# A retention layer and a bilinear feed-forward on one core: other zero products, wide state updates and a new order in the first pairs, and one burst two blocks sooner

## The chip, the core and the metric

The kernel runs on one core of a Trainium2 chip. A core has a matrix engine (TensorE, PE in the profile; its weight loads are listed apart as PEld), VectorE (DVE), ScalarE (ACT), GpSimd (POOL) and SyncE (SP), which here only issues transfers. Each engine works through its own queue in order and waits on semaphores that the others raise. Matmul results go to PSUM, from where DVE and ACT read them. The metric is device microseconds for one execution of the program.

## The reference

For 4 batches, 8 heads, 768 positions and head size 64, a recurrent layer keeps a 64x64 state for each head, and its output is the input of a bilinear feed-forward:

```
state = gamma[h] * state + outer(k[t], v[t])      # gamma[h] = 1 - 2**(-5-h)
y[t]  = q[t] @ state / sqrt(64)
x     = y, as 3072 tokens of 512 columns
out   = ((x @ w_a) * (x @ w_b)) @ w_out           # 512 -> 1536 -> 512
```

Inputs and output are float32.

## The kernel before

The 3072 tokens are 24 slots of 128. A slot is made of two chunks of 64 positions, and the recurrence is done chunk by chunk. The decay is put into tables with which k and q are scaled on their way to bf16 (`scaled`, L206). Then a chunk's output is the sum of two things: its masked scores times its values (`intra`), and the state of all earlier chunks times its queries (`inter`). The states are running sums of k-times-v products.

The feed-forward works on tiles of 4, 2, 2, 2, 2, 4, 4 and 4 slots (`TILES`, L16). For each of 12 column groups `ft` there is a product `a`, copied by ACT to bf16 (`asb`, L509), and a product `g`, which DVE multiplies by it into `ht` (L520); then twelve matmuls for each slot give `o` (L545), which ACT copies out. Weights come in six parts, cast by POOL. `a`, `g`, `o`, one of the two tiles of chunk sums and, in the first pairs, some transposes and scores take turns in a ring of three PSUM tiles ("ff", pool `psff`). A tile of the ring can be written only when the reader of the tile three places earlier is done. The other PSUM tiles are "y0", "y1", "at" (two banks) and "st".

The order of every engine's work is the order in which the program calls things: `seq` (L71) ties each instruction to the one before it on its engine. There are two ways in which slots are turned into columns of x.

*The first three pairs of slots (0 to 5)* go through functions ending in 2, called one by one from L559 to L637. A pair holds even positions in one slot and odd ones in the other (`par`). `casts2` scales k and q and casts v; `flip2` (L387) transposes k or q on TensorE into PSUM, and ACT or DVE copies the result to SBUF; `scores2` (L399) makes k-times-q with 64x64 matmuls; `mask2` (L415) is two DVE multiplications of 512 columns into `aT`; `update2` (L422) adds a chunk's k-times-v to the state in PSUM ("st") with sixteen 64x64 matmuls; `keep_state` (L439) has ACT copy its two halves into the off-diagonal-zero matrices `gbd[0]` or `gbd[1]`; `intra2` (L454) and `inter2` (L443) make the output in y0 and y1, or for pair 1 in two tiles of the ring; `leave2` (L466) copies the output's two halves into x, on ACT and DVE. Between these calls `warm` (L481) lets TensorE multiply zeros, for which `zero` (L125) is kept. When the first two pairs are through, the feed-forward of tile 0 begins on their four slots, in halves of 256 columns for ft 0 and 1, and the third pair is done among its blocks (L621 to L636).

*All later slots* go through `turn(new, old)` (L353), a burst of small matmuls that makes the states and scores of slots `new` and `new+1` and the outputs of `old` and `old+1`. The dictionary `ahead` (L640) says ahead of which feed-forward block each burst is called, as (tile, ft) or (tile, "o", slot). Its states use one "st" tile and one tile of the ring (L249); DVE adds four (sometimes three) running sums (L271), ACT casts them to `gst`, and the casts of outputs to x (L344) are put in a list `later` that is emptied ahead of the next `o` and, two at a time, after each block of a and g (L526, L537).

Of the kernel before, what the change touches and what calls it, by code (L numbers as in the profile page):

```python
# [23 lines left out]
def kernel(  # L24
# [100 lines left out]
    zero = const.tile([P, 2 * P], BF16, name="zero")  # L125
# [261 lines left out]
    def flip2(u, i, on, banks=None):  # L387
        into = (kT2, qT2)[i]
        if u not in into:
            into[u] = tra.tile([P, 2, HP, P], BF16, tag="kq"[i] + "T2", name="kq"[i] + "T2", bufs=2)  # L390
        for pars, eng in on:
            pool, tag = (psff, "ff") if banks is None else (psat, banks[pars[0]])
            tp = pool.tile([P, 2, HP, P], BF16, tag=tag, name="tp")[:, : len(pars)]
            for m, par in enumerate(pars):
                for hp in range(HP):
                    seq(nc.tensor.transpose(tp[:, m, hp, :], kqb[2 * u + par][:, i, hp, :, :], ident))  # L396
            cast(eng, into[u][:, pars[0] : pars[0] + len(pars)], tp)
# [17 lines left out]
    def mask2(u, par):  # L415
        t = 2 * u + par
        aT[t] = tra.tile([P, 2, HP, P], BF16, tag="aT", name="aT")
        for r in range(2):
            seq(nc.vector.tensor_tensor(aT[t][:, r], ats[t][r], masks[par].to_broadcast([P, HP, P]),  # L419
                                        op=ALU.mult))  # L420

    def update2(u, c, keep=True):  # L422
        if (u, c) == (PAIRS - 1, 1):
            return
        if (u, c) == (0, 0):
            state[0] = psst.tile([P, HP, D], F32, tag="st", name="st")
        st = state[0]
        for par in range(2):
            for hp in range(HP):
                for r in range(2):  # L430
                    t = 2 * u + par
                    seq(nc.tensor.matmul(st[half(r), hp, :], kb[t][half(c), hp, r, :],  # L432
                                         vb[t][half(c), HP * r + hp, :],
                                         start=((u, c, hp, par) == (0, 0, 0, 0)),
                                         stop=(hp == HP - 1), skip_group_check=True))
        if keep:
            keep_state(c)

    def keep_state(c):  # L439
        for r in range(2):  # L440
            seq(nc.scalar.copy(gbd[1 - c][half(r), :, half(r)], state[0][half(r), :, :]))
# [49 lines left out]
    def parts(J, ft, c0, c1):  # L491

        if J == 0 and ft in (2, 3):
            return [(c0, (c0 + c1) // 2), ((c0 + c1) // 2, c1)]
        return [(c0, c1)]

    def ffn_a(J, ft, c0=0, c1=None):
# [5 lines left out]
        for kt in range(KT):  # L503
            for b0, b1 in parts(J, ft, c0, c1):
                seq(nc.tensor.matmul(a[:, b0 - c0 : b1 - c0], wa_bf[:, kt, fs], xcols(J, kt, b0, b1),  # L505
                                     start=(kt == 0 and b0 == c0), stop=(kt == KT - 1 and b1 == c1),
                                     skip_group_check=True))
# [3 lines left out]
    def ffn_g(J, ft, c0=0, c1=None):  # L511
        c1 = TILES[J] * P if c1 is None else c1
        fs = slice(ft * P, (ft + 1) * P)
        g = psff.tile([P, 4 * P], F32, tag="ff", name="g")[:, : c1 - c0]
        for kt in range(KT):
            for b0, b1 in parts(J, ft, c0, c1):
                seq(nc.tensor.matmul(g[:, b0 - c0 : b1 - c0], wb_bf[:, kt, fs], xcols(J, kt, b0, b1),  # L517
                                     start=(kt == 0 and b0 == c0), stop=(kt == KT - 1 and b1 == c1),
                                     skip_group_check=True))
        seq(nc.vector.tensor_tensor(ht[J][:, ft, c0:c1], g, asbs.pop((J, ft, c0)), op=ALU.mult))  # L520
# [40 lines left out]
    casts2(1, {(K, 0): G_, (K, 1): G_, (Q, 0): G_})  # L561
# [59 lines left out]
    flip2(2, K, [((0, 1), A_)], ("y0",))  # L621
# [16 lines left out]
    for j in range(NO):  # L638
# [8 lines left out]
        (4, 0): [(casts, 17)], (4, "o", 0): [(turn, 14, 12), (casts, 18)],  # L647
# [57 lines left out]
```

## Time and profile before

The profiled execution is one of the program's executions, and its span is what the profile's times are counted in.

| | us |
|---|---|
| median of 3 runs | 226.02 |
| lowest of them | 225.84 |
| profiled execution | 226.63 |
| its span in the trace | 224.9 |
| TensorE busy in the span | 218.5 |
| DVE busy | 96.3 |
| ACT busy | 96.3 |
| POOL busy | 80.4 |

The page gives, for each engine, its busy time, and the busy share in forty slices of the span, 5.6 us each, as a digit in tenths. The timeline lists instructions in order of start, merged where they follow each other: start, length from the first start to the last end, engine, source line, operation, what it writes and reads, the number of them, and in brackets the idle time of the engine just before and who ended it. The end of a matmul is modelled, and matmuls overlap, so their prices are read from start to start. Span time 17.5 us is where the first matmuls of the feed-forward start; the burst at which the second part of the change aims begins at 115.18 us.

### The profile page before, as it was taken

The numbers are of one execution on the slowest core, as the hardware profiler recorded it, in microseconds if no ns is written. First come the engines' busy times: TensorE is split into PE (matmuls) and PEld (weight loads), VectorE is DVE, ScalarE is ACT, GpSimd is POOL, SyncE is SP. The second block draws the span as 40 slices with busy tenths as digits, with TensorE's granted clock in tenths as the row PEclk, the third lists the DMA queues.
The fourth block names the chain that finished last, engine by engine and source line by source line (L and its number), as shares of the span: only waits on it lengthen the run. The fifth ranks groups of instructions, "written<-read, shape, count | busy, mean of one in ns | idle before, by whom it ended". The sixth has DMA issues, their size and how long they took to land.

```text
span 224.9 us, 6284 instructions
## 1 busy us (share of the span) xinstructions
PE 218.5 (97%) x2632; PEld 133.5 (59%) x2632; DVE 96.3 (43%) x195; ACT 96.3 (43%) x207; POOL 80.4 (36%) x105
## 2 busy tenths in 40 slices
PE   8879999999999999999999999999999999999994
PEld 8768645686456866876875444554444544444443
DVE  3784347553406435472466333544343521334300
ACT  3475435433427426454457333355333354333221
POOL 5577798682544335350533535251000000000000
PEclk9999999999999999999999999999999999999999
DMA  6999999899999994988958899895100012100022
GB/s 179 347 379 383 365 314 407 260 206 194 228 243 271 222 223 80 223 222 186 212 135 194 127 226 239 187 235 146 47 0 0 3 50 93 47 3 1 0 93 95
DMA packets 96124, 39.72 MB, mean 177 GB/s; under 512 B 76000, under 2 KB 91616, under 8 KB 96096
## 3 DMA queue, kind: packets, MB, share of 16 engines
q1 hardware_dynamic: 95952, 39.20, 67.8%
q8 instruction: 20, 0.33, 0.6%
q10 hardware_dynamic: 144, 0.13, 0.2%
q14 instruction: 8, 0.07, 0.1%
HBM read 28.31 MB, written 6.29 MB: 154 GB/s over the span
## 4 chain that ended last, share of the span: by engine, by line
PE 96%; DVE 1%; issue 1%; ACT 0%
PE o L545 28%; PE a L505 28%; PE g L517 28%; PE idle L484 3%; PE y L321 1%; PE at L280 1%; PE y L333 1%; PE tp L396 1%; PE st L257 1%; PE y L449 1%; PE st L432 1%; DVE aT L419 1%; DVE kqb L212 1%; PE y L461 0%; PE at L409 0%
## 5 line engine op out<-in xcount | busy, mean ns | idle before, releaser
L520 DVE TENSOR_TENSOR ht<-g,asb 128x256 bf16<-128x256 f32 (+1 forms) x98 | 53.9, 550 | 84.2 <-PE g L517 74.3
L505 PE MATMUL a<-xt,wa_bf 128*128 128x256 bf16 (+1 forms) x400 | 77.6, 319 | 0.0
L517 PE MATMUL g<-xt,wb_bf 128*128 128x256 bf16 (+1 forms) x400 | 77.6, 319 | 0.0
L509 ACT CAST asb<-a 128x256 bf16<-128x256 f32 (+1 forms) x98 | 46.3, 473 | 71.2 <-PE a L505 71.2
L545 PE MATMUL o<-wo_bf,ht 128*128 128x512 bf16 (+2 forms) x312 | 64.4, 363 | 0.0
L505 PEld LDWEIGHTS <-wa_bf 128*128 128x128 bf16 x400 | 38.8, 98 | 24.0 <-DVE xt L184 0.4
L517 PEld LDWEIGHTS <-wb_bf 128*128 128x128 bf16 x400 | 39.0, 98 | 23.0
L545 PEld LDWEIGHTS <-ht 128*128 128x128 bf16 x312 | 28.8, 98 | 30.5
L212 POOL TENSOR_TENSOR kqb<-kf,ktab 128x512 bf16<-128x512 f32 x22 | 22.9, 1044 | 40.5 <-DMA kf<-in_k_dram 35.9
L182 ACT COPY osb<-o 128x512 f32<-128x512 f32 (+2 forms) x25 | 14.1, 565 | 32.9 <-PE o L545 27.6
L184 POOL CAST vb<-vf 128x512 bf16<-128x512 f32 x25 | 15.0, 613 | 24.0 <-DMA vf<-in_v_dram 21.6
L212 POOL TENSOR_TENSOR kqb<-qf,qtab 128x512 bf16<-128x512 f32 x21 | 22.3, 1066 | 0.0
L182 ACT CAST gst<-sums 128x256 bf16<-128x256 f32 x33 | 13.4, 405 | 6.3 <-DVE sums L271 3.0
L271 DVE TENSOR_TENSOR sums<-st,sums 128x256 f32<-128x256 f32 x30 | 12.7, 424 | 1.9 <-PE st L257 0.3
L286 DVE TENSOR_TENSOR aT<-at,mask 128x512 bf16<-128x512 f32 x18 | 11.5, 680 | 0.0
L484 PE MATMUL idle<-zero 128*128 128x170 bf16 (+1 forms) x56 | 8.1, 321 | 1.1 <-DVE zero L126 1.1
L344 ACT CAST xt<-y 128x512 bf16<-128x512 f32 x16 | 8.5, 584 | 0.0
L419 DVE TENSOR_TENSOR aT<-at,mask 128x512 bf16<-128x512 f32 x12 | 7.5, 681 | 0.4 <-PE at L409 0.4
L484 PEld LDWEIGHTS <-zero 128*128 128x128 bf16 x56 | 6.7, 130 | 1.3 <-DVE zero L126 1.1
L184 POOL CAST wb_bf<-wstb 128x1024 bf16<-128x1024 f32 (+1 forms) x7 | 6.4, 922 | 2.8 <-DMA wstb<-in_moe_w_b_dram 2.8
L184 POOL CAST wo_bf<-wsto 128x1024 bf16<-128x1024 f32 x6 | 6.3, 1043 | 2.8 <-DMA wsto<-in_moe_w_out_dram 2.8
L184 POOL CAST wa_bf<-wsta 128x1024 bf16<-128x1024 f32 (+1 forms) x7 | 6.4, 921 | 1.2 <-DMA wsta<-in_moe_w_a_dram 1.1
(53 smaller groups left out, 87.0 us busy)
## 6 DMA issues: line engine op xcount, KB each, us to landing
out_dram<-osb SPq DMA_DIRECT2D x23, 256.0 KB, 3.1
kf<-in_k_dram SPq DMA_DIRECT2D x18, 256.0 KB, 4.3
qf<-in_q_dram SPq DMA_DIRECT2D x18, 256.0 KB, 4.5
vf<-in_v_dram SPq DMA_DIRECT2D x18, 256.0 KB, 5.2
wsta<-in_moe_w_a_dram SPq DMA_DIRECT2D x6, 512.0 KB, 7.7
wstb<-in_moe_w_b_dram SPq DMA_DIRECT2D x6, 512.0 KB, 7.9
wsto<-in_moe_w_out_dram SPq DMA_DIRECT2D x6, 512.0 KB, 8.2
kf<-in_k_dram SPq DMA_DIRECT2D x3, 512.0 KB, 5.8
```

Source lines behind the costliest of these rows:

```text
L182: seq(nc.scalar.copy(dst, src))
L184: seq(engine.tensor_copy(dst, src))
L212: seq(eng.tensor_tensor(dst, src, tab, op=ALU.mult))
L271: seq(nc.vector.tensor_tensor(new, u[c][:, s], old, op=ALU.add))
L286: seq(nc.vector.tensor_tensor(aT[n][:, r].rearrange("p s h d -> p (s h) d"), at[:, r].rearrange("p s h d -> p (s h) d"), mask.to_broadcast ...
L419: seq(nc.vector.tensor_tensor(aT[t][:, r], ats[t][r], masks[par].to_broadcast([P, HP, P]), op=ALU.mult))
L484: seq(nc.tensor.matmul(idle[:, :w], zero[:, :P], zero[:, :w], start=True, stop=True, skip_group_check=True))
L505: seq(nc.tensor.matmul(a[:, b0 - c0 : b1 - c0], wa_bf[:, kt, fs], xcols(J, kt, b0, b1), start=(kt == 0 and b0 == c0), stop=(kt == KT - 1 a ...
L509: seq(nc.scalar.copy(asb, a))
L517: seq(nc.tensor.matmul(g[:, b0 - c0 : b1 - c0], wb_bf[:, kt, fs], xcols(J, kt, b0, b1), start=(kt == 0 and b0 == c0), stop=(kt == KT - 1 a ...
L520: seq(nc.vector.tensor_tensor(ht[J][:, ft, c0:c1], g, asbs.pop((J, ft, c0)), op=ALU.mult))
L545: seq(nc.tensor.matmul(o, ht[J][:, ft, i * P : (i + 1) * P], wo_bf[:, ft, c0:c1], start=(ft == 0), stop=(ft == NFT - 1)))
```

## The change

It has two parts. The first rewrites the calls for pairs 0 and 1:

- `zero` is twice as wide, and the zero products change: eight of 64 columns, two of 128 and four of 192 where there were eight, four and four of 256; two groups of three with 512 columns, written to "st", around pair 1's q transposes; the group of four ahead of the first state update is gone.
- `update2` uses eight matmuls of 64 rows by 128 columns with 128 columns moving. Each makes the products of two heads with each other as well, and the copies read the two blocks on the diagonal only. The state's PSUM tile is twice as wide.
- Pair 0's second q transposition is copied by ACT, not DVE. DVE, not POOL, scales the second k of pair 1. The first mask of pair 0 is done in two steps, with the scaling of pair 1's second q between them.
- Scores change places: for pair 0 and for pair 1 it is the second half whose scores are in the ring, and the first half's are in "at". Pair 1's q transposes use y0 and y1, and its output is one tile in "at" in place of two tiles of the ring.
- The order of calls: pair 1's first scores come ahead of update (0,0) and its second ones between `intra2(0,0)` and `intra2(0,1)`; `leave2(0)` on ACT comes ahead of update (0,1) and so ahead of its state copies; update (1,0) stands between `intra2(1,0)` and `intra2(1,1)`, and its two state copies are on ACT and DVE; the first `ffn_a` comes ahead of `inter2(1)`, and update (1,1) behind the second.
- `parts`, which split the matmuls of ft 2 and 3 of tile 0 into halves, is gone.

The second part moves `turn(14, 12)` from ahead of the first `o` of tile 4 to ahead of the block (4, 11), that is, ahead of its last a and g. The casts of slot 18 stay where they were.

```diff
-    zero = const.tile([P, 2 * P], BF16, name="zero")
+    zero = const.tile([P, 4 * P], BF16, name="zero")
...
-    def update2(u, c, keep=True):
+    def update2(u, c, on=(nc.scalar, nc.scalar)):
...
-            state[0] = psst.tile([P, HP, D], F32, tag="st", name="st")
+            state[0] = psst.tile([P, HP, P], F32, tag="st", name="st")
...
-                for r in range(2):
-                    t = 2 * u + par
-                    seq(nc.tensor.matmul(st[half(r), hp, :], kb[t][half(c), hp, r, :],
-                                         vb[t][half(c), HP * r + hp, :],
+                t = 2 * u + par
+                seq(nc.tensor.matmul(st[:, hp, :], kb[t][half(c), hp, :, :],
+                                     vb[t].rearrange("p (r hp) d -> p hp r d", r=2)[half(c), hp],
...
-            seq(nc.scalar.copy(gbd[1 - c][half(r), :, half(r)], state[0][half(r), :, :]))
+            cast(on[r], gbd[1 - c][half(r), :, half(r)], state[0][half(r), :, half(r)])
...
-    def intra2(u, par, begin, home=(psat, "y0", "y1")):
-        if begin:
-            ys[u] = [home[0].tile([P, HP, P], F32, tag=home[1 + c], name="y") for c in range(2)]
+    def intra2(u, par, begin, home=None):
+        if begin and home is None:
+            ys[u] = [psat.tile([P, HP, P], F32, tag=f"y{c}", name="y") for c in range(2)]
+        elif begin:
+            both = psat.tile([P, 2, HP, P], F32, tag=home, name="y")
+            ys[u] = [both[:, c] for c in range(2)]
...
-    casts2(1, {(K, 0): G_, (K, 1): G_, (Q, 0): G_})
+    casts2(1, {(K, 0): G_, (K, 1): D_, (Q, 0): G_})
...
-    warm(8, psat, "y1")
+    warm(8, psat, "y1", 64)
     flip2(0, Q, [((0,), A_)])
-    warm(4, psat, "y1")
-    flip2(0, Q, [((1,), D_)])
-    warm(4, psat, "y1")
-    scores2(0, 0, True)
-    scores2(0, 1)
+    warm(2, psat, "y1", P)
+    flip2(0, Q, [((1,), A_)])
+    warm(4, psat, "y1", 192)
+    scores2(0, 0)
+    scores2(0, 1, True)
+    mask2(0, 0, (0,))
     casts2(1, {(Q, 1): D_})
+    mask2(0, 0, (1,))
+    mask2(0, 1)
     flip2(1, K, [((0, 1), A_)])
-    flip2(1, Q, [((1,), A_), ((0,), A_)])
-    mask2(0, 0)
-    mask2(0, 1)
-    warm(4, psat, "y1")
+    warm(3, psst, "st", 4 * P)
+    flip2(1, Q, [((1,), A_), ((0,), A_)], ("y0", "y1"))
+    warm(3, psst, "st", 4 * P)
+    scores2(1, 0)
     update2(0, 0)
-    scores2(1, 0, True)
+    mask2(1, 0)
     intra2(0, 0, True)
+    scores2(1, 1, True)
+    mask2(1, 1)
     intra2(0, 1, False)
+    leave2(0, (A_, None))
     update2(0, 1)
-    leave2(0, (A_, None))
-    scores2(1, 1)
-    mask2(1, 0)
-    mask2(1, 1)
     inter2(0, True)
     leave2(0, (None, D_))
-    update2(1, 0)
-    intra2(1, 0, True, (psff, "ff", "ff"))
+    intra2(1, 0, True, "at")
+    update2(1, 0, (A_, D_))
     intra2(1, 1, False)
+    W2 = 2 * P
+    ffn_a(0, 0, 0, W2)
     inter2(1, True)
     leave2(1, (A_, D_))
-    W2 = 2 * P
-    ffn_a(0, 0, 0, W2)
-    update2(1, 1, False)
     ffn_a(0, 1, 0, W2)
+    update2(1, 1, None)
...
-        (4, 0): [(casts, 17)], (4, "o", 0): [(turn, 14, 12), (casts, 18)],
+        (4, 0): [(casts, 17)], (4, 11): [(turn, 14, 12)], (4, "o", 0): [(casts, 18)],
```

More of the change, by code (lines that the diff above doesn't have):

```diff
@@ L391, in flip2 @@
         for pars, eng in on:
-            pool, tag = (psff, "ff") if banks is None else (psat, banks[pars[0]])
+            pool, tag = (psff, "ff") if not banks or not banks[pars[0]] else (psat, banks[pars[0]])
             tp = pool.tile([P, 2, HP, P], BF16, tag=tag, name="tp")[:, : len(pars)]
@@ L413, in scores2, with mask2 @@
         ats[t] = at
-    def mask2(u, par):
+    def mask2(u, par, rows=(0, 1)):
         t = 2 * u + par
-        aT[t] = tra.tile([P, 2, HP, P], BF16, tag="aT", name="aT")
-        for r in range(2):
+        if t not in aT:
+            aT[t] = tra.tile([P, 2, HP, P], BF16, tag="aT", name="aT")
+        for r in rows:
             seq(nc.vector.tensor_tensor(aT[t][:, r], ats[t][r], masks[par].to_broadcast([P, HP, P]),
                                         op=ALU.mult))
-    def update2(u, c, keep=True):
+    def update2(u, c, on=(nc.scalar, nc.scalar)):
         if (u, c) == (PAIRS - 1, 1):
@@ L489 @@
     asbs = {}
[L491 to L495, printed above, removed]
     def ffn_a(J, ft, c0=0, c1=None):
@@ L503, in ffn_a @@
         for kt in range(KT):
[L504 to L507, printed above, removed]
+            seq(nc.tensor.matmul(a, wa_bf[:, kt, fs], xcols(J, kt, c0, c1),
+                                 start=(kt == 0), stop=(kt == KT - 1)))
         asb = asbs[J, ft, c0] = asbp.tile([P, 4 * P], BF16, tag="asb", name="asb")[:, : c1 - c0]
@@ L515, in ffn_g @@
         for kt in range(KT):
[L516 to L519, printed above, removed]
+            seq(nc.tensor.matmul(g, wb_bf[:, kt, fs], xcols(J, kt, c0, c1),
+                                 start=(kt == 0), stop=(kt == KT - 1)))
         seq(nc.vector.tensor_tensor(ht[J][:, ft, c0:c1], g, asbs.pop((J, ft, c0)), op=ALU.mult))
@@ L620 @@
             ffn_ab(0, ft)
-    flip2(2, K, [((0, 1), A_)], ("y0",))
+    flip2(2, K, [((0, 1), A_)], ("y0", None))
     ffn_a(0, 9)
```

11 lines of the change are left out of this document (5 added, 6 removed).

## The prediction

> **What bounds the kernel now.** I read the page from the top: the share of the span that each engine is busy, the forty slices with the granted clock, and the shares of the chain that ended last.
>
> ```profile
> span 224.9 us, 6284 instructions
> ...
> PE 218.5 (97%) x2632; PEld 133.5 (59%) x2632; DVE 96.3 (43%) x195; ACT 96.3 (43%) x207; POOL 80.4 (36%) x105
> ...
> PE   8879999999999999999999999999999999999994
> ...
> PEclk9999999999999999999999999999999999999999
> ...
> PE 96%; DVE 1%; issue 1%; ACT 0%
> ```
>
> TensorE is busy 97% of the span and carries 96% of the chain. Only the first three slices (16.9 us) and the last are below 9. So what can be won by order lies in the 6.4 us in which TensorE is idle: some 3 of them are the last slice, half empty behind the last matmul, 1 is ahead of the first matmul, and the other 2 to 3 are in the first pairs. After 17 us an edit costs or gains only what it adds to or takes from TensorE's own queue. The change sits in both places. I went on to the timeline of the first 22 us and of the burst at 115 us, and to the built order of both programs, for what each instruction waits on.
>
> **The change part by part.** A. The first two pairs, up to the matmuls of the first tile. These are the rows of the timeline on which the new order is laid out.
>
> ```profile
> 1.12 5.28 PE L484 MATMUL idle<-zero 128*128 128x170 bf16 x36 [1.12 <-DVE zero L126]
> 6.34 1.29 DVE L212 TENSOR_TENSOR kqb<-qf,qtab 128x512 bf16<-128x512 f32 x2 [0.18 <-DMA qf<-in_q_dram]
> 6.87 1.07 ACT L182 COPY kT<-tp 128x512 bf16<-128x512 bf16 x2 [1.86 <-PE tp L396]
> 6.98 1.04 PE L484 MATMUL idle<-zero 128*128 128x256 bf16 x8
> 7.86 0.39 PE L396 MATMUL tp<-ident,kqb 128*128 128x128 bf16 x4
> 7.90 2.04 POOL L212 TENSOR_TENSOR kqb<-kf,ktab 128x512 bf16<-128x512 f32 x2 [3.64 <-DMA kf<-in_k_dram]
> 8.28 0.59 ACT L182 COPY qT<-tp 128x512 bf16<-128x512 bf16 x1 [0.34 <-PE tp L396]
> 9.33 1.17 DVE L212 TENSOR_TENSOR kqb<-qf,qtab 128x512 bf16<-128x512 f32 x1
> 10.42 2.47 DVE L419 TENSOR_TENSOR aT<-at,mask 128x512 bf16<-128x512 f32 x4
> 11.57 1.18 ACT L182 COPY qT<-tp 128x512 bf16<-128x512 bf16 x2
> 12.50 0.44 PE L432 MATMUL st<-vb,kqb 64*64 64x64 bf16 x16
> 12.80 0.42 PE L409 MATMUL at<-qT,kT 64*64 64x128 bf16 x16
> 12.98 0.76 ACT L441 CAST gbd<-st 64x256 bf16<-64x256 f32 x2 [0.22 <-PE st L432]
> 13.26 2.52 DVE L419 TENSOR_TENSOR aT<-at,mask 128x512 bf16<-128x512 f32 x4 [0.37 <-PE at L409]
> 14.26 0.74 ACT L441 CAST gbd<-st 64x256 bf16<-64x256 f32 x2 [0.53 <-PE st L432]
> 15.03 0.73 ACT L182 CAST xt<-y 128x512 bf16<-128x512 f32 x1
> 15.73 0.22 PE L449 MATMUL y<-qT,gbd 128*64 128x128 bf16 x1 [0.94 <-issue]
> 15.87 0.37 PE L432 MATMUL st<-vb,kqb 64*64 64x64 bf16 x12
> 17.57 0.73 DVE L184 CAST xt<-y 128x512 bf16<-128x512 f32 x1 [0.85 <-PE y L449]
> 18.82 0.60 PE L517 MATMUL g<-xt,wb_bf 128*128 128x256 bf16 x4
> 19.25 1.04 PE L505 MATMUL a<-xt,wa_bf 128*128 128x256 bf16 x8
> ```
>
> And these are later rows of TensorE, for the price of a wide update and of a change of tile shape.
>
> ```profile
> 33.56 0.61 PE L396 MATMUL tp<-ident,kqb 128*128 128x128 bf16 x8
> 34.01 1.03 PE L505 MATMUL a<-xt,wa_bf 128*128 128x512 bf16 x4
> ...
> 36.92 0.42 PE L432 MATMUL st<-vb,kqb 64*64 64x64 bf16 x16
> 37.37 1.89 PE L505 MATMUL a<-xt,wa_bf 128*128 128x512 bf16 x8
> ```
>
> The wide update. Sixteen 64x64 matmuls become eight of 128 columns by 128. Sixteen ran in 0.42 us from the first start to the last end; a single matmul's record is about 0.2 us (15.73: 0.22), so they start within some 0.25 us: two at a time, one in each column half. A wide one fills both halves and has no partner. Its nearest row is the transposes: eight of 128 columns between 33.56 and 34.01, or 56 ns each, so 0.45 us. I take plus 0.2 us a call, five calls. The other end is zero, if a mode I don't see lets them overlap.
>
> The tile shape. After 16 starts in 0.25 us from 36.92, the next matmul of the full array starts only at 37.37, some 0.2 us late, where an ordinary one follows after 0.03 to 0.1. I take half of it, 0.1 us, a change. The wide update (64 rows by 128 columns) stands between 64x64 matmuls in the first pairs, so it adds about five changes, four on the chain below. The Trainium skill, "TensorEngine Tiling (Array Packing)", section Tiling Modes, says that changing the mode, and not only the tile, drains the engine; the late start at 37.37 agrees. It speaks against this change: with the full 0.2 us a change, term A would be plus 1.3 us, and with no price plus 0.5.
>
> The chain, in span time of the profiled run. Both q copies of pair 0 are now on ACT, behind two kT copies that end at 7.94, with 0.59 us each: 9.11, so the scores start near 9.2. The smaller filler matmuls let the q transposes come sooner but are otherwise hidden by this wait. The first mask follows 0.46 us behind the scores (12.80 to 13.26) and lasts 0.62 (2.47 in four): 10.25. Only then does DVE scale the second q of pair 1. The row at 9.33 shows 1.17 us for that, with POOL in its own scaling until 9.94; each of the two undisturbed ones at 6.34 took 0.65. POOL, with one k scaling less, starts its q scaling once q has landed (by 9.33) and is in it until about 10.4, so I take 0.9: 11.15 (ends 10.9 and 11.4). The k scaling that DVE takes over falls at 7.9, when the k tile has landed, in time that DVE has free. Transposing and copying q costs 0.42 to ACT's start (7.86 to 8.28), then 1.18: 12.75. The scores of pair 1 thus start at 12.80, as before. The two times three 512-column fillers, 0.65 us each, lie inside these waits.
>
> From here it lengthens. The update (0,0) now stands behind those scores: 0.28 for 16 of them, 0.1 for the shape, seven steps of 56 ns, 0.21 for the last, and 0.04 to ACT's start (12.94 to 12.98 before): the state copy runs 13.82 to 14.58, where it ran 12.98 to 13.74. Behind the copy TensorE waits with update (0,1), at about 14.68. On ACT the output copy of pair 0, 0.73 us, has been put ahead of the second state copy: it runs 14.8 to 15.53, after the matmuls of values with scores, and so the state copy is 15.55 to 16.31, not 14.26 to 15.00. Update (1,0) waits for it: 16.36, against 15.87. Copies of the state to ACT and then DVE (the built DVE instruction waits for ACT's) end at 17.8, but values, a shape change and the first a (0.44) fill TensorE until 17.84, so the 16 state-times-query matmuls run 17.84 to 18.41. Now the output copies of pair 1 don't run side by side, as DVE's did at 17.57 when it had waited for TensorE alone: they read one tile, and the DVE one is built to wait for ACT's. ACT 18.6 to 19.34, DVE 19.39 to 20.13. TensorE has a, wide update and g until 20.04, and the a of columns 256 to 511 can start at 20.18, against 19.25. So A is plus 0.9. DVE's masks (four by 0.62 from 13.26) end at 15.75 as before and cover nothing more; the weights were there sooner than any of this, since g ran at 18.82. If the mask, contention and shape prices all fall my way, A is plus 0.3; the worst of each gives plus 1.3.
>
> The pause. Just before update (1,0), TensorE stood 0.94 us in "issue", waiting for nothing in the trace, though the state copy had ended at 15.00. In the new order the same number of instructions is reached while it waits for ACT until 16.3, so a pause that comes back there costs nothing, and one that vanishes gains nothing: the cover is ACT's.
>
> B. The blocks ft 2 and 3 with whole 512-column matmuls: 16 in place of 32, same columns. Matmuls of 256 columns start 109 ns apart (four from 18.82 to 19.25), so two take 0.218 us; twelve of 512 columns fill 116.45 to 119.16 (below), at most 0.225 each. Zero. The columns that they needn't wait for in halves any more are long there, so no new wait.
>
> C. Update (2,0) at 36.92, in the stretch that TensorE bounds: plus 0.2 less what the shape change already costs there; I take plus 0.15, ends 0 and 0.25. Its waiting ACT copies are hidden behind two a blocks.
>
> D. The burst of slots 14/12, from behind the last a and g block of tile 4 to ahead of it.
>
> ```profile
> 115.18 0.28 PE L321 MATMUL y<-kqT,gst 64*64 64x64 bf16 x10
> 115.83 1.87 DVE L271 TENSOR_TENSOR sums<-st,sums 128x256 f32<-128x256 f32 x4
> 116.45 2.76 PE L545 MATMUL o<-wo_bf,ht 128*128 128x512 bf16 x12
> 118.05 1.07 ACT L344 CAST xt<-y 128x512 bf16<-128x512 f32 x2
> 119.16 0.32 PE L321 MATMUL y<-kqT,gst 64*64 64x64 bf16 x16
> ```
>
> The burst moves ahead of one a and one g, 0.43 us each (as from 18.82 to 19.25), to 114.31, and its matmuls are the same: 1.27 us (115.18 to 116.45). But it takes one of three turning PSUM tiles, and the third tile after it is now the first o of tile 4: the program shows this o waiting for the last of the four sums. These start 0.65 us into the burst (115.18 to 115.83), at 114.96, and take 1.87: 116.83. The o would start at 116.45 as before, and starts at 116.88: plus 0.43. The last ht is made after two masks (1.28) at 118.5; the last o matmul, at 119.26, needs it, so that is hidden. ACT now does the last asb (some 0.4) ahead of the rest, so its two output copies end near 119.5 and not at 119.12; the next burst reaches its banks at 119.55, so the bank wait that could be won (119.16, directly after ACT's end at 119.12) is not longer and was hardly there: below 0.1 us. No DMA moves: casts of slot 18 stay. D is plus 0.43, ends minus 0.1 and plus 0.6.
>
> The sum: 0.9 + 0 + 0.15 + 0.43 = plus 1.48 us. The profiled execution took 226.63 us with a span of 224.9, the median of the runs is 226.02; against the median, 227.5 us.
>
> **The rivals.** R1, the pause is worth something. It was 0.94 us on the chain, and it may be the fetching of TensorE's instructions, of which there are 112 fewer rows now. If it goes, to the full, on top of my lower end, A is 0.3 - 0.94 = minus 0.64; with C at 0.15 and D at 0.1 the time is 225.6. For it: "issue" with nothing awaited. Against: ACT's copies come later by themselves. The Trainium skill, "Runtime: NRT & Kernel Launch", section Instruction fetch mechanics, has instructions refilled in blocks of 256 at a cost that is mostly hidden; by that the pause would not be a refill, and R1 would gain nothing.
>
> R2, D hides: DVE takes the sums sooner or the o is not held. Then 227.0. Against: the wait stands in the built program.
>
> R3, the other side: slower by over 2%, or 4.5 us. The first 36 fillers took 147 ns for 170 columns, those at 6.98 took 109 ns for 256: half the rate until about 6.9 us. If the thinner filler between 7 and 9.2 (64 to 192 columns, not 256) lets the clock fall again, all TensorE work doubles until it returns. It decides only if this lasts through some 4.5 us of dense matmuls, from 17.5 to past 26: 231. Against: no gap in my layout is longer than 0.7 us, and the 0.94 us pause did not lower it.
>
> **How the numbers follow.** My forecast, plus 0.7 to plus 2.0, has 0.60, R1 0.22, R2 0.14, R3 0.04. The range goes from R1 with D at its lower end, 225.4, to the upper ends of A, C and D, plus 2.15 and 0.3 for what I haven't seen, 228.5; the forecast's own is 226.7 to 228.0. A change of 2% is about what a measurement of this kernel can tell from none; all but R3 lie within it, and no case reaches a gain of 4.5 us, since just 2 to 3 us of idle time can be ordered away. I leave 0.01 for that.
>
> **What would show it.** Right: the wide st matmuls about 56 ns apart; the a of the second half of the first tile near 20.2; DVE's second xt copy behind ACT's; a gap of 0.4 us ahead of the first o of tile 4 near 117.8, released by sums. Wrong: that a before 19.3, o directly behind g, or a lower clock after 7 us.

## The result, and the profile after

The changed kernel took 227.65 us (median of 3 runs, 227.45 to 227.87) where the kernel before took 226.02: a ratio of 1.0082, with an interval of 1.0059 to 1.0105. One of the three runs of before took 283.55 us and is not in the ratio, which is of fast runs alone. The forecast was 227.5, in a range of 225.4 to 228.5. The profiled execution of the changed kernel took 227.87 us, that of before 226.63.

From the page of the kernel after, the span, the busy times, TensorE's forty slices and the shares of the chain:

```profile
span 226.1 us, 6153 instructions
...
PE 217.5 (96%) x2556; PEld 131.0 (58%) x2576; DVE 97.0 (43%) x196; ACT 95.8 (42%) x207; POOL 79.8 (35%) x104
...
PE   7799999999999999999999999999999999999993
...
PE 91%; DMA 2%; DVE 2%; ACT 2%; issue 1%; SPq 0%; DVEq 0%
```

TensorE is still the bound. The first two slices have gone from 8 to 7, the third from 7 to 9 and the last from 4 to 3; the rest is as it was. (Some twenty records of matmuls are missing here, as 2556 matmuls beside 2576 weight loads show.) The page alone doesn't say where 1.2 us of span went; the timeline does. First the opening of the kernel after:

```profile
9.86 1.19 DVE L212 TENSOR_TENSOR kqb<-qf,qtab 128x512 bf16<-128x512 f32 x1
12.67 0.42 PE L409 MATMUL at<-qT,kT 64*64 64x128 bf16 x16 [0.29 <-ACT qT L182]
13.02 0.62 PE L432 MATMUL st<-vb,kqb 64*128 64x128 bf16 x8
13.67 0.76 ACT L182 CAST gbd<-st 64x256 bf16<-64x256 f32 x2 [1.05 <-PE st L432]
14.47 0.74 ACT L182 CAST xt<-y 128x512 bf16<-128x512 f32 x1
14.48 0.60 PE L432 MATMUL st<-vb,kqb 64*128 64x128 bf16 x8
15.12 0.74 ACT L182 CAST gbd<-st 64x256 bf16<-64x256 f32 x2
15.92 0.60 PE L432 MATMUL st<-vb,kqb 64*128 64x128 bf16 x8
17.34 0.64 PE L450 MATMUL y<-qT,gbd 128*64 128x128 bf16 x16
18.02 0.74 ACT L182 CAST xt<-y 128x512 bf16<-128x512 f32 x1 [0.20 <-PE y L450]
18.80 0.74 DVE L184 CAST xt<-y 128x512 bf16<-128x512 f32 x1 [1.35 <-ACT xt L182]
19.00 0.61 PE L512 MATMUL g<-xt,wb_bf 128*128 128x256 bf16 x4
19.59 1.03 PE L502 MATMUL a<-xt,wa_bf 128*128 128x256 bf16 x8
```

The reader is to see a chain that hands over between TensorE and ACT: wide update (13.02), state copy (13.67), wide update (14.48), state copy (15.12), wide update (15.92). At its end stand the two output copies in a row (18.02 and 18.80); the second ends at 19.54, and the a of the tile's second half starts at 19.59. A release that follows the end of its releaser by 0.04 us is a link of the chain: the copy at 13.67 starts 0.03 us behind the update's end (13.64), the update at 14.48 starts 0.05 us behind the copy's (14.43).

Then the moved burst, in the timeline of the kernel after:

```profile
114.89 0.28 PE L321 MATMUL y<-kqT,gst 64*64 64x64 bf16 x10
115.54 1.87 DVE L271 TENSOR_TENSOR sums<-st,sums 128x256 f32<-128x256 f32 x4
116.61 0.60 PE L512 MATMUL g<-xt,wb_bf 128*128 128x256 bf16 x4
117.47 2.76 PE L539 MATMUL o<-wo_bf,ht 128*128 128x512 bf16 x11 [0.26 <-DVE sums L271]
```

The four sums end at 117.41 and the first o of tile 4 starts at 117.47, with TensorE idle for 0.26 us before it and DVE's sums named as what ended the wait.

The way through the span, from the timelines of three executions (the third is the same changed kernel, profiled a second time):

| us of span time | before | after | after, again |
|---|---|---|---|
| first scores of pair 1 | 12.80 | 12.67 | 13.26 |
| a of tile 0's second half | 19.25 | 19.59 | 20.16 |
| a behind update (2,0) | 37.37 | 37.86 | 38.44 |
| first a of tile 5 | 123.28 | 124.06 | 124.76 |
| end of the last matmul | 221.59 | 222.37 | 223.07 |
| span | 224.9 | 226.1 | 226.7 |

Differences between rows give the parts. From the scores to a: 6.45 us before, 6.92 and 6.90 after (plus 0.47 and 0.45). From there to the a behind update (2,0): 18.12, 18.27 and 18.28 (plus 0.15 and 0.16). From there to tile 5: 85.91, 86.20 and 86.32 (plus 0.29 and 0.41). From there to the last matmul: 98.31 in all three. What comes ahead of the scores differs between two executions of one kernel by 0.59 us, more than the change itself does there. The last matmul is thus 0.78 or 1.48 us later than in the profiled execution of before; behind it, the span is another 0.4 us longer in the first execution of after (3.76 us from the last matmul to the end, where before has 3.33 and the second execution of after 3.61), in the landing of the last output.

### The profile page after: what moved, and what is told of

It reads as the page before. It is cut to its first block, busy times and chain, and to the rows that moved or that the text cites. A ratio compares the mean times of both kernels' runs of the same rounds, so it can differ in the third digit from the quotient of the medians.

```text
span 226.1 us, 6153 instructions
## 1 busy us (share of the span) xinstructions
PE 217.5 (96%) x2556; PEld 131.0 (58%) x2576; DVE 97.0 (43%) x196; ACT 95.8 (42%) x207; POOL 79.8 (35%) x104
## 4 chain that ended last, share of the span: by engine, by line
PE 91%; DMA 2%; DVE 2%; ACT 2%; issue 1%; SPq 0%; DVEq 0%
PE a L502 28%; PE g L512 28%; PE o L539 27%; DMA qf<-in_q_dram 2%; PE y L321 1%; PE at L280 1%; PE y L333 1%; PE st L257 1%; ACT qT L182 1%; PE st L432 1%; PE tp L396 1%; DVE kqb L212 1%; DVE sums L271 1%; PE at L409 1%; PE y L465 1%
## 5 line engine op out<-in xcount | busy, mean ns | idle before, releaser
L539 PE MATMUL o<-wo_bf,ht 128*128 128x512 bf16 (+2 forms) x299 | 62.7, 362 | 1.6 <-issue 1.0
L502 PEld LDWEIGHTS <-wa_bf 128*128 128x128 bf16 x392 | 37.8, 98 | 24.9 <-DVE xt L184 0.4
L512 PEld LDWEIGHTS <-wb_bf 128*128 128x128 bf16 x392 | 38.1, 98 | 23.8
L212 POOL TENSOR_TENSOR kqb<-kf,ktab 128x512 bf16<-128x512 f32 x21 | 22.3, 1064 | 42.2 <-DMA kf<-in_k_dram 41.9
L488 PE MATMUL idle<-zero 128*128 128x170 bf16 (+4 forms) x55 | 7.2, 298 | 1.3 <-DVE zero L126 1.3
L298 DVE COPY lgr<-bq 128x1 f32<-128x1 f32 x4 | 0.6, 154 | 15.1 <-PE y L321 15.1
```

What stands on the lines that cost most here:

```text
L212: seq(eng.tensor_tensor(dst, src, tab, op=ALU.mult))
L502: seq(nc.tensor.matmul(a, wa_bf[:, kt, fs], xcols(J, kt, c0, c1), start=(kt == 0), stop=(kt == KT - 1)))
L512: seq(nc.tensor.matmul(g, wb_bf[:, kt, fs], xcols(J, kt, c0, c1), start=(kt == 0), stop=(kt == KT - 1)))
L539: seq(nc.tensor.matmul(o, ht[J][:, ft, i * P : (i + 1) * P], wo_bf[:, ft, c0:c1], start=(ft == 0), stop=(ft == NFT - 1)))
```

## The experiments

Unless told otherwise, a ratio is against runs of the kernel before on the same chip, with its interval.

**The changed kernel again, and its parts.** Four kernels ran together: the changed one once more; before with only the burst moved; after with only the burst left where it was; and before with only the wide update. The edits are those of the change itself; the matmuls of the last one, to which the wider "st" tile and copies of its diagonal blocks belong, are

```diff
-                for r in range(2):
-                    seq(nc.tensor.matmul(st[half(r), hp, :], kb[t][half(c), hp, r, :],
-                                         vb[t][half(c), HP * r + hp, :],
+                seq(nc.tensor.matmul(st[:, hp, :], kb[t][half(c), hp, :, :],
+                                     vb[t].rearrange("p (r hp) d -> p hp r d", r=2)[half(c), hp],
```

The changed kernel again:

> The changed kernel unaltered, beside the kernel before, with more rounds. First theory, the terms of the traces: TensorE's last matmul came 0.78 us later in span time than in the kernel before (pairs 0.34, wide update among the blocks 0.20, burst 0.24 net), and 0.42 us of the profiled 1.24 was the landing of the last output; so 0.8 to 1.2 us slower. Rival, something that differs between executions and not in these terms, such as when the clock is released in the first 7 us: 1.6 us slower or more, as the three runs shown, with spans that scatter by over 0.4 us.

Only the burst:

> The kernel before with only the burst of slots 14/12 moved to ahead of (4, 11). First theory, the ring of three PSUM tiles: the first o of tile 4 waits 0.4 us for the last of the four sums, as in the changed kernel, so 0.2 to 0.45 us slower (the lower end if the following burst is shorter by 0.2 us again). Rival, the shorter following burst pays for the wait: within 0.1 us of the kernel before.

Only the pairs, wide updates among them:

> The changed kernel with the burst of slots 14/12 back ahead of the first o of tile 4. First theory: what is left is the pairs (0.34 in the traces) and the wide update among the blocks (0.20), so 0.4 to 0.8 us slower than the kernel before, and no gap at that o. Rival, that nearly all of the loss is in the burst: within 0.2 us of the kernel before. Second rival, that the pairs cost more than the one profiled execution shows, since its clock came up 1.8 us sooner than in the kernel before: 1.0 us slower or more.

Only the wide updates:

> The kernel before with only the update of the state made wide (eight matmuls of 64 rows by 128 columns in place of sixteen of 64 by 64; the copies read the blocks on the diagonal). First theory: update (2,0) costs 0.2 us, and those in the first pairs 0.2 us each where they are on the chain, two or three of them, less what the 0.94 us pause covers: 0.3 to 0.7 us slower. Rival, the pause ahead of update (1,0) depends on the number of TensorE instructions before it, goes away with them, and pays for the wide matmuls: 0.2 us slower to 0.5 us faster.

Measured, with 225.99 us for before:

| kernel | median us | ratio | interval |
|---|---|---|---|
| after, again | 227.70 | 1.0071 | 1.0049 to 1.0093 |
| only the burst moved | 226.29 | 1.0009 | 0.9995 to 1.0022 |
| only the pairs changed | 227.15 | 1.0041 | 1.0028 to 1.0054 |
| only the wide update | 226.79 | 1.0028 | 1.0010 to 1.0045 |

The loss of the whole repeats, and most of it is in the pairs: 1.2 us by the medians, with 0.3 by itself for the burst (its interval still holds no difference) and 0.55 for it on top of the pairs. The width alone costs 0.8 us in the order of before; its ratio of 1.0028 puts it nearer 0.6. The first theories for the whole (0.8 to 1.2) and for the pairs (0.4 to 0.8) were too low: they came from one profiled execution of before, of which more below. In the timeline of the kernel with only the wide update:

```profile
12.42 0.62 PE L431 MATMUL st<-vb,kqb 64*128 64x128 bf16 x8
12.97 0.42 PE L409 MATMUL at<-qT,kT 64*64 64x128 bf16 x16
15.32 0.62 PE L431 MATMUL st<-vb,kqb 64*128 64x128 bf16 x8
```

From the wide update to the scores behind it are 0.55 us, where before had 0.30 (12.50 to 12.80), though there are half as many matmuls. And a thing that was not looked for: the last row is update (1,0), and it starts at 15.32, straight behind the state copy that ends at 15.26. In the execution of before it had waited until 15.87, behind 0.94 us in "issue". The pause was not there. (A stall of the same kind stands later in this execution; it comes up further down.)

**The width taken back.** After, with sixteen 64x64 matmuls an update and all else as changed:

```diff
-                seq(nc.tensor.matmul(st[:, hp, :], kb[t][half(c), hp, :, :],
...
+                for r in range(2):
...
+                    seq(nc.tensor.matmul(st[half(r), hp, :], kb[t][half(c), hp, r, :],
```

> The kernel after with the five state updates back to sixteen 64x64 matmuls each; its orders and the moved burst stay. If the width is dear by itself (eight wide starts 56 ns apart and two changes of tile shape a call, as widening alone cost 0.8 us in the median), about 0.8 us below the kernel after, near 226.9, and the first g of 256 columns about 0.7 sooner than its 19.00. If in the new order the wide matmuls lie in waits for ACT and the order is what costs, only 0.1 to 0.3 below, near 227.5.

Measured: 226.87 us, ratio 1.0036 (1.0023 to 1.0049), 0.8 below the changed kernel. (The changed kernel did not run beside this one and the next three, where before took 226.08; the comparison is with its 227.65 and 227.70.) In its timeline:

```profile
12.64 0.42 PE L409 MATMUL at<-qT,kT 64*64 64x128 bf16 x16
12.86 0.35 PE L433 MATMUL st<-vb,kqb 64*64 64x64 bf16 x11
13.35 0.76 ACT L182 CAST gbd<-st 64x256 bf16<-64x256 f32 x2 [0.75 <-PE st L433]
14.15 0.44 PE L433 MATMUL st<-vb,kqb 64*64 64x64 bf16 x16 [0.17 <-ACT gbd L182]
18.27 0.73 DVE L184 CAST xt<-y 128x512 bf16<-128x512 f32 x1 [1.39 <-ACT xt L182]
19.05 1.03 PE L503 MATMUL a<-xt,wa_bf 128*128 128x256 bf16 x8
```

From the scores to the first state copy are 0.71 us, not 1.00, and to the a of the second half 6.41, not 6.92. Half a microsecond is in these rows, and the row of output copies hides some more: g starts at 18.30 here, and a only 0.75 us later, behind DVE's output copy that ends at 19.00, where four matmuls of 256 columns take 0.43 (18.82 to 19.25 in before). Behind these rows is update (2,0), in the timeline of before and in that of the kernel after:

```profile
36.45 0.64 PE L409 MATMUL at<-qT,kT 64*64 64x128 bf16 x32
```

```profile
36.74 0.64 PE L409 MATMUL at<-qT,kT 64*64 64x128 bf16 x32
37.31 0.62 PE L432 MATMUL st<-vb,kqb 64*128 64x128 bf16 x8
37.86 1.90 PE L502 MATMUL a<-xt,wa_bf 128*128 128x512 bf16 x8
```

The wide call has 0.55 us to the next matmul there, and the narrow one of before had 0.45 (36.92 to 37.37). The step into it, from the start of the scores, is 0.57 us and not 0.47. Together that is 0.20. The width is dear by itself, in either order.

**The burst between a and g.** The moved burst is put between the last a and the last g of tile 4. Then the first o is the second tile of the ring behind the burst, and no longer the third:

```diff
         ffn_a(J, ft)
+        if (J, ft) == (4, 11):
+            turn(14, 12)
         ffn_g(J, ft)
...
-        (4, 0): [(casts, 17)], (4, 11): [(turn, 14, 12)], (4, "o", 0): [(casts, 18)],
+        (4, 0): [(casts, 17)], (4, "o", 0): [(casts, 18)],
```

> The kernel after with the burst of slots 14/12 between the last a and the last g of tile 4, so that the third tile of the ring behind it is the second o and not the first. If the 0.4 us ahead of the first o is the wait for the last of the four sums, it goes: 0.4 us below the kernel after, near 227.25, the first o of tile 4 directly behind g, and no wait of o for sums. If the burst costs because its shape changes and the ACT copies stand elsewhere, no difference: 227.65.

Measured: 227.04 us, ratio 1.0039 (1.0026 to 1.0053), 0.6 below the changed kernel. In its timeline:

```profile
116.28 1.87 DVE L271 TENSOR_TENSOR sums<-st,sums 128x256 f32<-128x256 f32 x4 [0.48 <-PE st L257]
116.90 0.61 PE L512 MATMUL g<-xt,wb_bf 128*128 128x256 bf16 x4
117.56 2.56 PE L541 MATMUL o<-wo_bf,ht 128*128 128x512 bf16 x11
```

The sums end at 118.15. The row of o has eleven of twelve matmuls; the first one's record is missing. Its weights were loaded without a wait:

```profile
117.24 2.15 PEld L541 LDWEIGHTS <-ht 128*128 128x128 bf16 x11
```

So o ran directly behind g, ahead of the end of the sums. From the start of the last g but one to tile 5 are 9.33 us (114.66 to 123.99), where before has 9.50 and the two executions of after 9.70 and 9.75. The moved burst's loss is the wait of one PSUM tile, as the built program showed. By the times alone it could be doubted, since the interval touches that of the changed kernel (1.0049 to 1.0093).

**Two PSUM tiles for pair 1's output.** DVE's output copy waits for ACT's because both read one tile. Here the first half has the tile "y0", which is free by then:

```diff
-            ys[u] = [both[:, c] for c in range(2)]
+            ys[u] = [psat.tile([P, HP, P], F32, tag="y0", name="y"), both[:, 1]]
```

> The kernel after with the two output halves of pair 1 in two PSUM tiles, so that DVE's copy no longer waits for ACT's. By the prediction's layout (the copies in a row set when the second half of a can start) DVE's copy starts near 18.05 and not 18.80, and up to 0.6 us is won: 227.1. If TensorE has work until then anyway (in the trace of after, a, a wide update and g fill 17.91 to 19.44, and the second half of a starts at 19.59), at most 0.15 is won: 227.5.

Measured: 227.48 us, ratio 1.0059 (1.0045 to 1.0072). In its timeline:

```profile
17.73 0.74 ACT L182 CAST xt<-y 128x512 bf16<-128x512 f32 x1
17.96 0.73 DVE L184 CAST xt<-y 128x512 bf16<-128x512 f32 x1 [0.58 <-PE y L450]
19.39 1.04 PE L502 MATMUL a<-xt,wa_bf 128*128 128x256 bf16 x8
```

The two copies run side by side now and DVE's ends 0.25 us before g even starts (18.69 against 18.94), but a comes only 0.13 us sooner, counted from the scores (12.60 to 19.39, or 6.79). TensorE had a wide update and g to do. That the copies stood in a row was real, and nearly hidden; the medians put it at 0.2, which the intervals can't tell from nothing. With narrow updates it is hidden no longer: there, as the rows above show, a waits some 0.3 us for DVE's copy.

**The first update ahead of the scores**, as before has it:

```diff
-    scores2(1, 0)
     update2(0, 0)
+    scores2(1, 0)
```

> The kernel after with the first state update ahead of the scores of pair 1, where the kernel before has it; all else as after. If the state's chain (update, copy, update, copy) sets the end of the first pairs, its first copy starts 0.8 us sooner (12.8 and not 13.67) and 0.3 to 0.7 us are won: 227.0 to 227.3. If the masks of DVE and TensorE's own work set it, the scores of pair 1 start later by 0.1 to 0.5 and nothing is won, or 0.2 lost: 227.6 to 227.9.

Measured: 227.26 us, ratio 1.0057 (1.0044 to 1.0069). In its timeline:

```profile
12.60 0.62 PE L432 MATMUL st<-vb,kqb 64*128 64x128 bf16 x8
13.15 0.42 PE L409 MATMUL at<-qT,kT 64*64 64x128 bf16 x16
13.26 0.76 ACT L182 CAST gbd<-st 64x256 bf16<-64x256 f32 x2 [0.48 <-PE st L432]
19.56 1.03 PE L502 MATMUL a<-xt,wa_bf 128*128 128x256 bf16 x8
```

The first state copy starts 0.66 us behind the update, at 13.26 and not 13.67, and the scores start at 13.15 and not 12.67. From the first scores of pair 0 (9.00 here, 8.79 in after) to that a are 10.56 us, and 10.80 in after: some 0.2 less in the trace, and 0.4 by the medians, as the first theory had it. The intervals (1.0044 to 1.0069, and 1.0049 to 1.0093 for after) overlap, so the size stays open.

**All four together**: narrow, the burst between a and g, two tiles, the first update first.

> The kernel after with the four changes of the last runs together: narrow updates, the first update ahead of the scores of pair 1, two PSUM tiles for pair 1, the burst between the last a and g of tile 4. If the four losses are separate, they add up to 0.8 + 0.4 + 0.2 + 0.6 = 2.0 below the kernel after, 225.7, and no more is left of the change than its 0.3 below before. If they share one chain (state copy, update, copy), the first three give about 1.0 together, and it ends at 226.1, as before.

Measured: 226.06 us where before took 226.13 beside it, ratio 0.9999 (0.9982 to 1.0016). In its timeline:

```profile
18.86 0.82 PE L503 MATMUL a<-xt,wa_bf 128*128 128x256 bf16 x6
```

That is what the second theory gave: the four losses are not separate. By the time of the whole program nothing is left of the loss, and what the change keeps besides (other zero products, pair 0's q copies on ACT, a k scaling on DVE, masks and scores in new places, whole matmuls for ft 2 and 3) makes no difference that can be measured. The opening alone shows more. From the first state update to the a are 6.35 us here (12.51 to 18.86). Three executions with before's opening that hold the pause told of below have 6.49 to 6.75, and one that holds none has 5.97 (12.46 to 18.43, only the burst moved). So where the pause is missing, some 0.4 us of the opening may still be lost, and how often it is missing the runs without a profile don't show.

**Two tries for less than before.** Before with nothing but the burst between a and g, and the same with both q scalings of pair 1 on DVE:

```diff
-    casts2(1, {(K, 0): G_, (K, 1): G_, (Q, 0): G_})
+    casts2(1, {(K, 0): G_, (K, 1): G_})
...
-    casts2(1, {(Q, 1): D_})
+    casts2(1, {(Q, 1): D_, (Q, 0): D_})
```

> The kernel before with nothing but the burst of slots 14/12 moved between the last a and the last g of tile 4. If the moved burst costs only by the wait of the first o for the sums, nothing is left: 226.0 as before, or 0.1 below (from the first a behind update (2,0) to the first a of tile 5 that order took 85.81 us, before 85.91). If the place itself is worse, 226.3 as when the burst alone was moved ahead of both.

> The kernel before with the burst between a and g and with both q scalings of pair 1 on DVE, one behind the other, in place of one on DVE and one on POOL at the same time (1.17 and 1.49 us in the trace of before, where DVE alone took 0.65). If that contention sets the scores of pair 1, they start up to 0.5 us sooner than 12.77, and the time is 225.5 to 225.8. If ACT's copies of k and q (2.2 us in a row) or the masks that DVE does 0.3 later set them, no gain or a loss of up to 0.3: 226.0 to 226.3.

Measured beside 226.13 for before: 225.85, ratio 0.9996 (0.9977 to 1.0014), and 226.97, ratio 1.0040 (1.0021 to 1.0060). The first is the same as before. The second lost, for a reason that neither theory had. In its timeline:

```profile
9.37 1.75 DVE L212 TENSOR_TENSOR kqb<-qf,qtab 128x512 bf16<-128x512 f32 x2 [0.58 <-DMA qf<-in_q_dram]
11.04 1.88 DVE L419 TENSOR_TENSOR aT<-at,mask 128x512 bf16<-128x512 f32 x3
11.77 0.38 PE L396 MATMUL tp<-ident,kqb 128*128 128x128 bf16 x4 [1.35 <-DVE aT L419]
```

Both q are scaled by 11.12, and TensorE transposes them only at 11.77: their PSUM tile comes free with the first mask of pair 0, which DVE now does behind the second scaling. The scores of pair 1 start at 13.43. The size of that loss is open: the twelve runs scatter from 226.42 to 227.63, about the 226.59 of the profiled one. No version beats before.

**The pause, looked at again.** The kernel before, unchanged, for one more profile:

> The kernel before, unchanged, for a second profile of its first 16 us. In two of the three profiles so far that have its opening order, TensorE stood 0.94 and 0.68 us in issue before the last state-times-query matmul of pair 0, and in both the first load of the instruction queue fell at 13.2 to 13.5 us; in the third it fell at 11.5 and the pause was missing. If the late load makes the pause, a load before 12.5 goes with no pause and a last matmul near 221.0, and one behind 13 with a pause of 0.5 us or more at the same matmul and a last matmul near 221.6. A pause without a late load, or a late load without a pause, speaks against it.

Measured: 226.57 us for the profiled execution; the median was 226.20 beside 225.75 for the same program (ratio 1.0014, 1.0000 to 1.0028), which shows how far two sets of runs of one kernel can lie apart. TensorE's rows in its timeline, and the row of the instruction queue in its transfers between 13 and 16 us:

```profile
14.37 0.41 PE L449 MATMUL y<-qT,gbd 128*64 128x128 bf16 x7
15.48 0.22 PE L449 MATMUL y<-qT,gbd 128*64 128x128 bf16 x1 [0.70 <-issue]
```

```profile
q8 instruction: 1, 0.02, 1.8%
```

And in the execution of before with only the burst moved, whose opening is the same, the same matmuls, and the queue's row between 10 and 13 us:

```profile
14.34 0.41 PE L449 MATMUL y<-qT,gbd 128*64 128x128 bf16 x8
15.02 0.38 PE L432 MATMUL st<-vb,kqb 64*64 64x64 bf16 x12 [0.27 <-ACT gbd L441]
```

```profile
q8 instruction: 1, 0.02, 1.9%
```

In the first, seven of eight matmuls run, then 0.70 us of nothing, then the eighth. In the second all eight run together, and the next wait is for ACT. Where the load of the instruction queue fell between 13 and 16 us there was the pause, at the same matmul each time (before, 0.94; before again, 0.70; before with the burst between a and g, 0.68); where it fell between 10 and 13 there was none (three other kernels with that opening or nearly that, and all eight profiles with the new one). The last matmul came at 221.53, as the late load was expected to go with. That late loads and pauses go together at this place is shown.

There is a second such place. In the timeline of the kernel with only the wide update, and in that of before, again:

```profile
120.80 0.31 PE L280 MATMUL at<-kqT 64*64 64x64 bf16 x14 [0.75 <-issue]
```

```profile
119.55 0.35 PE L257 MATMUL st<-vb,kqb 64*64 64x64 bf16 x18 [0.25 <-issue]
```

The two stalls stand at different instructions, scores in one and a state update in the other. But counted in the traces, 1630 weight loads of TensorE lie ahead of each. At that count before has 0.27 us between two weight loads (119.34 to 119.61) and the four together 0.34; in after and its second execution there is nothing. A stall that keeps its place in the count, and not in the program, fits a load of instructions better than a wait for data. That the load makes the stall is still a reading: it was not tried to move a load by itself.

## Why the prediction was right, and where it was not

The forecast was 1.48 us above before; 1.63 to 1.71 were measured in two comparisons. The range held it, and the side and the size were right. By its own steps:

*A, the first pairs, plus 0.9.* The direction and the links were right: q copies on ACT, then the mask, then a contended q scaling on DVE (0.9 forecast, between the 0.65 of an undisturbed one and the 1.17 of before; 1.19 measured at 9.86, and 1.45 in the second execution), scores near 12.80 (12.67), the first state copy a full microsecond behind them, the last two output copies in a row. The scores came in time even so, since the first mask started 0.4 us sooner than laid out (9.26, not 9.66). The layout has 7.38 us from the scores to the a of the second half; 6.92 and 6.90 were measured. The step that failed is the output copy of pair 0 "put ahead of the second state copy", which by the prediction held it until 15.55. The layout starts that copy 2.00 us behind the scores and has the state copy wait for its end. In the trace it starts 1.80 us behind them, beside the wide update at 14.48, and the state copy at 15.12 follows the update's end (15.08) and not the copy's (15.21). That is 0.3 of the 0.46 us (2.75 and 2.45 us from the scores to the state copy); the rest is spread over links of 0.1 us and less.

*The pause, nothing.* This is the second failure, and it has the other sign. The prediction called it covered, since ACT would be late anyway, and put A against an execution that held it. It was no fixed part of the kernel: without it, the same opening takes 5.66 us from the scores to a (12.77 to 18.43 with only the burst moved), not 6.45. Against that the new opening costs 1.25 us, and 0.47 against the profiled execution. The median of before, 226.02, lies 0.6 below its profiled execution, and the prediction took that distance off without asking what it was made of. Whether the pause is part of it stays open: of three profiled executions with the pause, two took 226.57 and 226.63, but the third (the burst between a and g) 225.95, near its kernel's median of 225.85. So two errors, A too long by 0.46 and before's opening too slow by the pause, went against each other. That the time came out so near is luck: with A at the 0.47 that was measured, the same sum gives 227.1.

The prediction weighed the pause by the Trainium skill, "Runtime: NRT & Kernel Launch", section Instruction fetch mechanics: refills of 16 KiB whose cost is mostly hidden. The loads here are 0.02 MB each, which agrees, but in three of the profiles such a load goes with 0.68 to 0.94 us that nothing hides. These rows speak against the sentence that "by that the pause would not be a refill".

*R1.* Its first half came true: in no profile of the new opening was there a pause. It was the price that was wrong: what was gained there was spent on wide updates and a longer chain, and A didn't stay at its lower end.

*The wide update.* Plus 0.2 a call, and 0.1 a change of shape. Eight wide starts, with 0.62 us from the first start to the last end and some 0.22 for a single one, are (0.62 - 0.22) / 7 = 57 ns apart, where 56 were forecast. The 0.22 is the mean of the kernel after's group of these matmuls:

```profile
L432 PE MATMUL st<-vb,kqb 64*128 64x128 bf16 x40 | 3.1, 216 | 0.2
```

The change of shape shows in the steps into the wide call: 0.35 us from the start of sixteen scores (12.67 to 13.02) where the narrow update follows after 0.22 (12.64 to 12.86), and 0.57 against 0.47 ahead of update (2,0). That is some 0.1 a change, as forecast. By the medians the five calls make 0.8, in either order, about half of the whole loss. It was the dearest single edit, and the prediction never put its five calls together in one sum: they stand spread over A and C.

*B* and *C*, zero and plus 0.15: together 0.15 and 0.16. Apart, they are some minus 0.04 and plus 0.20: from the a of the second half to the a behind update (2,0) are 18.08 us with narrow updates in the new order (19.05 to 37.13), 18.12 in before and 18.27 to 18.28 in after.

*D, plus 0.43.* Mechanism and size of the wait were right. The sums were forecast to start 0.65 us into the burst and the o 2.57 us behind its start; they are at 0.65 (114.89 to 115.54) and 2.58 (117.47). From the last g but one to tile 5, 0.20 and 0.25 us of that remain (9.50, 9.70, 9.75). What was missed is the next burst: in before it holds the 0.27 us behind 1630 weight loads, and in after nothing stands there. The order that takes the wait of o away gives 0.37 and 0.42 back. R2, that it hides, fell. *R3*, a lower clock, did not come: the page grants the full clock in every slice (the last section says what that leaves out of the first 7 us), and the dense matmuls of 256 columns start 0.11 us apart, as in before.

Of the signs that were named, the wide starts, DVE's copy behind ACT's (18.80 behind 18.76) and the gap ahead of the first o, released by sums, came as told. The a of the second half came at 19.59 and not near 20.2; in the second execution it came at 20.16, but from scores that were 0.6 later, so that isn't the sign either. (The chances of the prediction add up to 1.01, a slip of 0.01.)

## What to carry to other kernels

A stall that the profile puts down to "issue" may belong to that one execution; three of six profiles of this opening, or nearly this one, had it. Profile the kernel before twice ahead of summing against it. Half as many matmuls need not be less time: here sixteen 64x64 products started within some 0.25 us, and eight wide ones, half of whose results nobody reads, within 0.40. And when a block of work is moved that takes a tile of a rotating ring, count what comes as many places later as the ring has tiles; one place decides whether a wait is there.

## What was not expected of the hardware

The same zero products of 170 columns, 32 of the first 36, took different times from one execution to the next. In the timeline of before:

```profile
1.66 4.74 PE L484 MATMUL idle<-zero 128*128 128x170 bf16 x32
```

and in that of before with only the burst moved:

```profile
1.66 3.94 PE L484 MATMUL idle<-zero 128*128 128x170 bf16 x32
```

The page shows a full granted clock in both. But in the first all of them start 0.14 us apart; in the second they do so until 4.6 us and are 0.07 apart from then on. The trace's record of the granted clock begins at 6.90 us in the first and at 4.61 in the second, and the page counts the time ahead of the record as full. In after the rows have 4.12 us, and 4.74 in its second execution, with a record from 5.11 and from 6.79.

The three executions with the pause are those of their opening, or nearly theirs, in which the faster starts begin last (6.3 to 6.9 us; without the pause 4.5 to 5.9). So a late clock goes with the pause as a late load does, and which of them comes first isn't shown; in the second execution of after the clock was as late, and there was no pause. The scores of pair 1 don't follow the clock in before (12.80 and 12.77). In after they came 0.6 us later with the late clock, but there k had landed later as well: DVE's first k scaling waited for it until 5.22 and not 4.88. Why the record begins at 4.6 us once and near 7 another time, the runs don't show.
